# Seven half products for chunk 6, its sums on VectorE, and fewer weight sums per AV group

## The chip, the cores and the metric

One core of a Trainium2 chip runs the whole program. The metric is the device time of one execution in microseconds; the kernel before has a median of 409.77 us over three runs. TensorE (PE) multiplies matrices, VectorE (DVE), ScalarE (ACT) and GpSimd (POOL) work elementwise, and DMAs are issued by SyncE (SP), ACT and POOL.

## The reference

An attention whose queries are averaged in pairs, and then a gated feed-forward network on its output:

```python
q_pool = q.reshape(B, H, S // 2, 2, D).mean(axis=3)        # B=8, H=8, S=1152, D=64
scores = scale * np.matmul(q_pool, k.transpose(0, 1, 3, 2))
attn = np.exp(scores - np.max(scores, axis=-1, keepdims=True))
attn = attn / (np.sum(attn, axis=-1, keepdims=True) + 1e-09)
attn_out = np.matmul(attn, v)                               # (8, 8, 576, 64)
x = attn_out.transpose(0, 2, 1, 3).reshape(4608, 512)
h = (x @ w1) * (x @ w2) @ w3                                # 512 -> 1024 -> 1024
out = h @ w_out                                             # (4608, 512), float32
```

## The kernel before

**Attention.** Heads are worked on in 32 pairs. POOL casts keys, pooled queries and values to fp16; they are turned on TensorE for the first pairs and by DMA later. The scores of all pairs are one long row that is cut into 324 steps of 512 columns for two heads (`scores`, L434); ACT takes the exponential of each step into a ring in SBUF (L448). An AV group (`av_mm`, L461) multiplies a ring section of 128 queries with the values; a column of constants beside the values gives the sum of the exponentials. VectorE takes its reciprocal into `rzall` and scales (`av_norm`, L491). There are 144 such groups (`UNITS`). The result goes into `xT`.

**Network.** `w3 @ w_out` does not depend on the tokens: it is computed once into `T16` (`t_groups`, L544), 128 rows at a time, each in two steps of eight matmuls on 256 columns. The 4608 tokens are nine chunks of 512. For chunks 0 to 6 `moe_groups` (L613) makes, for each of eight blocks `ft` of 128 hidden features, the product with w1, which is kept (`keep`), and the product with w2, which VectorE multiplies with it (`gate`, L664) into the tile `g`. Then `g` is multiplied with T.

For chunks 0 to 5 that last product is done in seven half-sized products instead of eight, in the manner of Strassen and Winograd (`product`, L630): `g` and T are seen as 2 x 2 blocks, sums and differences of blocks of `g` are made by POOL (`sums`, L651, and `minus`, L731), those of T once by `t_sum`. Each half product is eight matmuls on 256 columns. Product 1 comes after block 4, and the other six wait in `late_fills` and run among the next chunk's steps. Results are added up on VectorE and stored quarter by quarter. Chunk 6 takes the plain way (L706): four token tiles, each eight matmuls on 512 columns, evicted half by VectorE and half by ACT.

Chunks 7 and 8 (`late_chunks`, L770) come when attention is over. They use seven products for the projections too, with sums of the weights (`weight_sums`, L734; eight POOL instructions, `wS`) and of `xT` (`x_sums`, L757; four POOL instructions for each chunk, `xS`). Their order (`LATE_ORDER`), the PSUM bank of each unit (`LATE_PLACES`) and the queue of some stores (`LATE_BY_ACT`) are written out by hand. The third unit uses the bank `avb`.

**Order.** Every engine runs its instructions in the order in which the program issues them. The 324 score steps are 108 visits of three (`VS`). What stands after the scores of a visit (AV groups `A`, network steps `m` or `s` by the PSUM bank they use, turns `P`) is chosen by `_visits` (L184), a search with a cost model over the list `fills` of the steps' sizes; a half product or a projection has size 1, a full token tile size 2. `av_step` (L1029) issues an AV group, its turn and its norm, and then one weight sum, as long as `todo` has any. After the last visit:

```python
while avn[0] < NU:          # L1076
    av_step()
    ...
    fill(avn[0] != NU - 4)
tail[0] = True              # L1083
```

Then come both sets of `x_sums` on POOL (L1089), a range test of all reciprocals on VectorE (L1094 to L1102, tile `ok`), the steps that are left (`while fill()`, L1103), a matmul that counts the test's results into `avb` (L1105) and VectorE's read of it (`badi`, L1107). If a value was out of range, a general version runs instead; with these inputs none is. With `tail` set, ACT instead of VectorE evicts the w1 products.

**Start.** Fifteen matmuls on the identity run into `avb` (L945) before the first data is there.

Of the kernel before, what the change touches and what calls it, by code (L numbers as in the profile page):

```python
# [258 lines left out]
    "0703 g31640 o00205 o01511 o10476 o11302"  # L259
).split()  # L260
LATE_ON_DVE = "o11c11".split()
LATE_BY_ACT = "o00c21 o01c12 o10c12 o10c21 o11c12 o11c21".split()


@with_exitstack
def kernel(
# [277 lines left out]
    def t_groups():  # L544
        w3T = {}

        def turn(ft):
            def go(pt):
                w3T[ft] = msb.tile([128, NF, 128], FP16, tag="t2k", bufs=2, name="w3T")
                ph = pt.bitcast(FP16)  # L550
                for a in range(NF):
                    nc.tensor.transpose(ph[:, a * 128:a * 128 + 128],
                                        w3c[ft // 4][:, ft % 4, a * 128:a * 128 + 128], ident16)

            return 0.5, go, lambda pt: nc.vector.tensor_copy(out=w3T[ft].rearrange("p a i -> p (a i)"),
                                                             in_=pt.bitcast(FP16)), W3_AT[ft // 2]

        def mult(ft, n0):
            def go(pT):
                for a in range(NF):  # L560
                    nc.tensor.matmul(pT[:, 0:256], w3T[ft][:, a, :], wosb[:, a, n0:n0 + 256],  # L561
                                     start=(a == 0), stop=(a == NF - 1))

            return 1, go, lambda pT: nc.vector.tensor_copy(out=T16[:, ft, n0:n0 + 256], in_=pT[:, 0:256]), WO_AT
# [48 lines left out]
    def moe_groups(c):  # L613
        t = {}
        lagged, late_fills[:] = late_fills[:], []
        seven = c < LATE - 1

        def first(pa, ft):
            if ft == 0:
# [22 lines left out]
        def quarter(h, n, pt, x):  # L642
            osb = msb.tile([128, 2, HM], FP32, tag="osb", bufs=3, name="osb")
            plus(osb, pt, x)
            store_two(nc.gpsimd, c * CH + h * HC, osb, slice(n * HM, n * HM + HM))

        def p1(pt):
            t["p"] = msb.tile([128, 2, HM], FP32, tag="t2k", bufs=2, name="p")
            nc.vector.tensor_scalar_mul(out=t["p"], in0=two(pt), scalar1=IS)

        def sums(f, n):  # L651
            g = t["g"]
            if f == 0:
                t["s1"] = msb.tile([128, HF, HC], FP16, tag="s1", bufs=1, name="s1")
            fs = slice(f, f + n)
            s1, a11, a21, a22 = t["s1"][:, fs], g[:, fs, 0:HC], g[:, fs, HC:CH], g[:, HF + f:HF + f + n, HC:CH]
            nc.gpsimd.tensor_tensor(out=s1, in0=a21, in1=a22, op=ALU.add)  # L657
            minus(a21, a11, a21)
            minus(a11, s1, a11)

        def half(fts):
            for ft in fts:
                def gate(pb, ft=ft):
                    nc.vector.tensor_tensor(out=t["g"][:, ft, :], in0=pb, in1=t["a"], op=ALU.mult)  # L664
# [11 lines left out]
        if seven:  # L676
            yield 1, lambda pt: product(pt, t["g"][:, 0:HF, 0:HC], 1), p1, 0.0
        yield from half(range(HF + 1, NF))
        if seven:
            g = t["g"]  # L680
            lo, hi = slice(0, HC), slice(HC, CH)

            def p2(pt):
                quarter(0, 0, pt, t["p"])
                for f in range(0, HF, 2):
                    minus(g[:, HF + f:HF + f + 2, lo], g[:, HF + f:HF + f + 2, lo], g[:, f:f + 2, lo])

            def p7(pt):
                t["z"] = msb.tile([128, 2, HM], FP32, tag="t2k", bufs=2, name="z")
                plus(t["z"], pt, t["p"])  # L690

            def p5(pt):
                t["bank"] = pt
                product(pt, t["s1"], 5)

            late_fills.extend((
                (1, lambda pt: product(pt, g[:, HF:NF, lo], 2), p2, 0.0),
                (1, lambda pt: product(pt, g[:, 0:HF, lo], 6), lambda pt: plus(t["p"], pt, t["p"]), 0.0),
                (1, lambda pt: product(pt, g[:, 0:HF, hi], 7), p7, 0.0),
                (1, lambda pt: product(pt, g[:, HF:NF, hi], 4), lambda pt: quarter(1, 0, pt, t["z"]), 0.0),  # L700
                (1, p5, lambda pt: quarter(1, 1, pt, t["z"]), 0.0),
                (1, lambda pt: product(t["bank"], g[:, HF:NF, lo], 3, False),
                 lambda pt: quarter(0, 1, t["bank"], t["p"]), None),
            ))
            return
        for tt in range(0, CH, 128):  # L706
            def go(po, tt=tt):
                for ft in range(NF):
                    nc.tensor.matmul(po, t["g"][:, ft, tt:tt + 128], T16[:, ft, :],  # L709
                                     start=(ft == 0), stop=(ft == NF - 1))  # L710

            def put(po, tt=tt):
                osb = msb.tile([128, dm], FP32, tag="osb", bufs=3)
                if tail[0]:
                    nc.vector.tensor_scalar_mul(out=osb[:, 0:256], in0=po[:, 0:256], scalar1=1.0 / (SCL * SCL))
                    nc.scalar.mul(out=osb[:, 256:512], in_=po[:, 256:512], mul=1.0 / (SCL * SCL))
                else:
                    nc.vector.tensor_scalar_mul(out=osb, in0=po, scalar1=1.0 / (SCL * SCL))
                if c == LATE - 1:
                    cut = 128 if tt < 256 else 64  # L720
                    for r in range(0, 128, cut):
                        for n in range(0, dm, 128):
                            store(nc.sync, c * CH + tt, osb[r:r + cut, n:n + 128], slice(n, n + 128), slice(r, r + cut))
                else:
                    store(nc.sync if c == LATE - 2 else nc.gpsimd, c * CH + tt, osb)

            yield 2, go, put, 0.0

    wS, tS, xS, todo = [], {}, {}, []

# [26 lines left out]
    def x_sums():  # L757
        for c in (0, 1):
            st = att.tile([128, 4, NC // 2, HC], FP16, tag="qst", name="xS")
            (_, a, n), = runs(LATE + c)  # L760
            b11, b12 = xT[:, 0:NC // 2, a:a + HC], xT[:, 0:NC // 2, a + HC:a + n]
            b21, b22 = xT[:, NC // 2:NC, a:a + HC], xT[:, NC // 2:NC, a + HC:a + n]
            x1, x2, x3, x4 = (st[:, i] for i in range(4))
            minus(x1, b12, b11)
            minus(x2, b22, x1)
            minus(x3, b22, b12)
            minus(x4, b21, x2)
            xS[c] = {1: b11, 2: b21, 3: b22, 4: x4, 5: x1, 6: x2, 7: x3}

    def late_chunks(before_end):  # L770
        room = att.tile([128, 27, 512], FP32, tag="ring", bufs=1, name="room")
# [170 lines left out]
        out=ident16, in_=ident16, compare_op=ALU.not_equal, fill=1.0,  # L942
        base=0, channel_multiplier=1, pattern=[[-1, 128]],
    )
    for _ in range(15):  # L945
        nc.tensor.matmul(avb[:, 0:64], ident16, ident16[:, 0:64], start=True, stop=True)
    for t in kq16s:
        nc.gpsimd.memset(t[QT:128, NB - 1], 0.0)
    nc.gpsimd.memset(half, 0.0)
# [55 lines left out]
                      ((old * FLAT + RING + TO[t]) // G) // VS - 1))  # L1005
    fills = []
    for ft in range(0, NF, 2):
        fills += [(0.5, W3_AT[ft // 2], "ms")] * 2 + [(1, WO_AT, "ms")] * 4
    free = []
    for n in range(NU + 1):  # L1010
        for c in loose.get(n, []):
            step = [(1, 0.0, "ms")]
            rest = step * 4 + [(1, 0.0, "m")] * 2
            fills += step * LAG + (rest if c else []) + step * (2 * NF - LAG)
            fills += step if c < LATE - 1 else [(2, 0.0, "ms")] * (CH // 128)
        free.append(len(fills))
    turn = {}
    for p in range(1, NPE):
# [10 lines left out]
    def av_step():  # L1029
        i = avn[0]  # L1030
        avn[0] += 1
        av_mm(i)
        if on_pe(i - 1):
            x_turn(i - 1)
        av_norm(i)
        if on_pe(i - 1):
            x_copy(i - 1)
        p, t = UNITS[i]
        if p >= XD and t == QM - 1:
            x_dma(p)  # L1040
        weight_sum()
        release()

    seen = -1
# [57 lines left out]
    nc.vector.memset(ones, 1.0)  # L1102
    while fill():  # L1103
        pass
    nc.tensor.matmul(avb[0:1, 0:1], okh, ones, start=True, stop=True)  # L1105
    badi = const.tile([1, 1], mybir.dt.int32)
    nc.vector.tensor_scalar(out=badi, in0=avb[0:1, 0:1], scalar1=-1.0, scalar2=float(128 * NQ),  # L1107
# [37 lines left out]
```

## Time and profile before

| | us |
|---|---|
| median of 3 runs | 409.77 (409.23 to 409.91) |
| the profiled execution | 409.23 |
| its span in the trace | 407.6 |
| TensorE busy | 392.2 |
| ACT busy | 336.6 |
| POOL busy | 282.0 |
| VectorE busy | 230.8 |
| granted TensorE clock | 0.998 |

Busy time is the time in which an engine executes an instruction. Matmuls are pipelined, so their mean duration is longer than the distance from one to the next; the chain of waits shows the distances. Times in rows are microseconds from the start of the span, durations behind them microseconds or nanoseconds as the view says. Tile names stand as `out<-in`.

### The profile page before, as it was taken

What the parts mean: (1) busy time and instruction counts of PE and PEld (TensorE: products, weight loads), DVE (VectorE), ACT (ScalarE), POOL (GpSimd) and SP (SyncE); (2) the same over time, 40 slices, a digit from 0 to 9 for tenths busy, and PEclk for the clock granted to TensorE, in tenths of its full rate; (3) what the DMA queues carried; (4) which work ended last, traced back from release to release, by engine and by line L of the source; (5) the groups of instructions that cost most, each with busy time, mean ns of one, the idle gap of its engine ahead of it and who ended that gap; (6) DMA issues with size and microseconds to landing.
All of it is one profiled execution on the core that took longest, in us unless ns stands there. A gap on an engine that the chain in (4) does not pass through costs nothing.

```text
span 407.6 us, 13533 instructions
## 1 busy us (share of the span) xinstructions
PE 392.2 (96%) x5632; PEld 275.5 (68%) x5632; DVE 230.8 (57%) x610; ACT 336.6 (83%) x384; POOL 282.0 (69%) x319
## 2 busy tenths in 40 slices
PE   4899999999999999999999999999999999999995
PEld 2477877665676666756676668666877767548884
DVE  1255665565555555465556555655555456845993
ACT  4989998999999999999999899989998987027752
POOL 5889975993968358855786398649663799930860
PEclk9999999999999999999999999999999999999999
DMA  8999998999889997999979999999896402311005
GB/s 260 253 321 285 276 291 296 348 252 276 167 272 261 260 209 183 319 219 254 296 217 303 268 214 218 220 319 277 187 282 133 62 16 66 79 55 49 2 27 185
DMA packets 94001, 86.37 MB, mean 212 GB/s; under 512 B 60272, under 2 KB 68720, under 8 KB 93936
## 3 DMA queue, kind: packets, MB, share of 16 engines
q1 hardware_dynamic: 83888, 59.06, 59.9%
q0 software_dynamic: 8896, 25.11, 22.2%
q10 hardware_dynamic: 1152, 1.31, 1.0%
q8 instruction: 44, 0.72, 0.7%
q14 instruction: 21, 0.17, 0.1%
HBM read 67.11 MB, written 9.44 MB: 188 GB/s over the span
## 4 chain that ended last, share of the span: by engine, by line
PE 89%; ACT 4%; POOL 3%; DVE 2%; issue 1%; DMA 1%; ACTq 0%; POOLq 0%
PE psc L443 20%; PE avb L474 17%; PE mo L587 12%; PE mot L587 9%; PE b L811 7%; PE mo L633 6%; ACT ring L448 3%; PE mo L561 3%; PE mot L633 3%; PE avb L471 2%; PE b L587 2%; PE b L709 2%; PE ptk L383 2%; POOL wS L747 2%; PE mo L811 1%
## 5 line engine op out<-in xcount | busy, mean ns | idle before, releaser
L448 ACT ACTIVATE ring<-psc 128x1024 f16<-128x1024 f32 x324 | 307.8, 1027 | 29.0 <-PE psc L443 27.4
L443 PE MATMUL psc<-kqT 64*128 64x512 f16 (+7 forms) x1152 | 97.6, 291 | 5.1 <-ACT ring L448 2.2
L474 PEld LDWEIGHTS <-ring 128*128 128x128 f16 x2304 | 84.0, 98 | 22.3 <-issue 8.8
L474 PE MATMUL avb<-vaug,ring 128*128 128x65 f16 x2304 | 91.5, 194 | 0.0
L443 PEld LDWEIGHTS <-kqT 64*128 64x128 f16 x1152 | 46.8, 95 | 34.3 <-issue 12.7
L355 POOL CAST kq<-kst 128x1152 f16<-128x1152 f32 x31 | 35.6, 1148 | 23.5 <-issue 12.6
L495 DVE RECIPROCAL rzall<-avb 128x2 f32<-128x2 f32 x144 | 23.9, 166 | 47.0 <-PE avb L474 21.5
L657 POOL TENSOR_TENSOR s<-gT 128x256 f16<-128x256 f16 (+1 forms) x18 | 14.9, 828 | 37.5 <-DVE gT L664 27.9
L359 POOL TENSOR_TENSOR kq<-qst 128x512 f16<-128x512 f32 x31 | 39.4, 1270 | 1.3 <-DMA qst<-in_q_dram 1.3
L664 DVE TENSOR_TENSOR gT<-mo,asb 128x512 f16<-128x512 f32 x35 | 24.2, 691 | 26.1 <-PE mo L587 24.9
L368 POOL CAST vaug<-vst 128x1152 f16<-128x1152 f32 x32 | 36.6, 1143 | 0.8 <-DMA vst<-in_v_dram 0.6
L587 PE MATMUL mo<-xT,w2sb 128*128 128x512 f16 (+2 forms) x160 | 36.2, 354 | 0.0
L587 PEld LDWEIGHTS <-w1sb 128*128 128x128 f16 x256 | 22.7, 98 | 19.7 <-issue 3.0
L587 PEld LDWEIGHTS <-w2sb 128*128 128x128 f16 x256 | 21.7, 97 | 19.9 <-issue 4.1
L633 PEld LDWEIGHTS <-gT 128*128 128x128 f16 x288 | 26.3, 98 | 8.5 <-issue 3.9
L509 DVE TENSOR_TENSOR xb<-avb,rzall 128x128 f16<-128x128 f32 x96 | 28.0, 292 | 3.3
L732 POOL TENSOR_TENSOR gT<-gT 128x512 f16<-128x512 f16 (+1 forms) x30 | 28.6, 963 | 1.5
L587 PE MATMUL mot<-xT,w1sb 128*128 128x512 f16 (+1 forms) x124 | 27.8, 352 | 0.0
L628 DVE COPY asb<-mo 128x512 f32<-128x512 f32 x25 | 17.3, 692 | 16.6 <-PE mo L587 16.3
L587 PE MATMUL mo<-xT,w1sb 128*128 128x512 f16 (+1 forms) x116 | 25.9, 351 | 0.0
L628 DVE COPY asb<-mot 128x512 f32<-128x512 f32 x27 | 18.7, 692 | 5.0 <-PE mot L587 5.0
L901 POOL TENSOR_TENSOR room<-gT 128x512 f16<-128x512 f16 x6 | 6.8, 1155 | 18.7 <-PE b L811 17.4
(159 smaller groups left out, 553.4 us busy)
## 6 DMA issues: line engine op xcount, KB each, us to landing
vst<-in_v_dram SPq DMA_DIRECT2D x25, 576.0 KB, 5.0
kst<-in_k_dram SPq DMA_DIRECT2D x23, 576.0 KB, 5.7
qst<-in_q_dram SPq DMA_DIRECT2D x23, 512.0 KB, 6.7
kst<-in_k_dram POOLq DMA_DIRECT2D x8, 576.0 KB, 10.1
qst<-in_q_dram POOLq DMA_DIRECT2D x8, 512.0 KB, 10.7
out_dram<-osb POOLq DMA_DIRECT2D x16, 256.0 KB, 5.2
vst<-in_v_dram POOLq DMA_DIRECT2D x7, 576.0 KB, 7.0
w3c<-in_moe_w_dram POOLq DMA_DIRECT2D x4, 512.0 KB, 8.3
```

The source lines that it names most:

```text
L355: nc.gpsimd.tensor_copy(out=kq16[:, 0:NJ].rearrange("p c u d -> p u c d"), in_=kst.rearrange("p u (c d) -> p u c d", d=D))
L359: eng.tensor_tensor(out=kq16[:, NJ:NJ + QM].rearrange("p c u d -> p u c d"), in0=qv[:, :, :, 0], in1=qv[:, :, :, 1], op=ALU.add)
L368: nc.gpsimd.tensor_copy(out=va[:, :, :, 0:D], in_=vs.pop(p).rearrange("p u (c d) -> p u c d", d=D))
L443: nc.tensor.matmul(psc[:, u, f - s * G:f - s * G + ln], kT2[u * 64:u * 64 + 64, jt, :], qpT[u * 64:u * 64 + 64, i0:i0 + ln], start=True, s ...
L448: nc.scalar.activation(out=ring[:, :, r0:r0 + G], in_=psc, func=AF.Exp, bias=0.0, scale=SCALE)
L474: nc.tensor.matmul(avb[:, o + u * E1:o + u * E1 + E1], ring[:, u, c0:c0 + 128], va[:, u, jt, :], start=(jt == 0 and u == 0), stop=(jt == N ...
L509: nc.vector.tensor_tensor(out=xbt, in0=av[:, :, 0:D], in1=rzall[:, i, :].unsqueeze(2).to_broadcast([128, 2, D]), op=ALU.mult)
L587: nc.tensor.matmul(pw[:, d0:d0 + n], wt[:, mc, ft * 128:ft * 128 + 128], xT[:, mc, a:a + n], start=(mc == 0 and d0 == 0), stop=(mc == NC - ...
L628: nc.vector.tensor_copy(out=t["a"], in_=pa)
L633: nc.tensor.matmul(pt[:, u * HM:u * HM + HM], a[:, f, u * 128:u * 128 + 128], tS[n][:, f, :], start=(start and u == 0 and f == 0), stop=(f ...
L732: nc.gpsimd.tensor_tensor(out=out, in0=x, in1=y, op=ALU.subtract)
L811: nc.tensor.matmul(pt[:, n * f:n * f + n], l[:, i, :], b[:, i, :], start=(p in (1, 5) and f == 0 and i == 0), stop=(i == kc - 1), skip_gro ...
```

## The change

- Chunk 6 is multiplied with T by seven half products. All of them come after block 7, in the order 1, 2, 6, 7, 5, 4, 3. Its sums are issued to VectorE behind the gates of blocks 5 (three on 512 columns), 6 and 7 (three each on 256 columns) and are written to the free tiles `kq16s`; the last difference (`s4`) stays on POOL. ACT evicts product 1. Its four quarters are stored in 32 pieces, 28 issued by SP and 4 by ACT.
- A weight sum follows every second AV group.
- `x_sums` for the second late chunk is issued after chunk 6's steps.
- The last store (`o01c12`) is issued by SP.
- The fifteen matmuls at the start are gone.
- In `t_groups` row block 3 is one step of eight matmuls on 512 columns with one eviction. The list `fills` has one entry of size 2 there, and seven of size 1 for chunk 6's product.

```diff
-LATE_BY_ACT = "o00c21 o01c12 o10c12 o10c21 o11c12 o11c21".split()
+LATE_BY_ACT = "o00c21 o10c12 o10c21 o11c12 o11c21".split()
...
-        def mult(ft, n0):
+        def mult(ft, n0, w=256):
             def go(pT):
                 for a in range(NF):
-                    nc.tensor.matmul(pT[:, 0:256], w3T[ft][:, a, :], wosb[:, a, n0:n0 + 256],
+                    nc.tensor.matmul(pT[:, 0:w], w3T[ft][:, a, :], wosb[:, a, n0:n0 + w],
                                      start=(a == 0), stop=(a == NF - 1))
...
-            for n in range(4):
-                yield mult(ft + n // 2, n % 2 * 256)
+            yield mult(ft, 0)
+            yield mult(ft, 256)
+            if ft != 2:
+                yield mult(ft + 1, 0)
+                yield mult(ft + 1, 256)
+            else:
+                yield mult(ft + 1, 0, dm)
...
-        seven = c < LATE - 1
+        final = c == LATE - 1
...
             plus(osb, pt, x)
-            store_two(nc.gpsimd, c * CH + h * HC, osb, slice(n * HM, n * HM + HM))
+            if not final:
+                store_two(nc.gpsimd, c * CH + h * HC, osb, slice(n * HM, n * HM + HM))
+                return
+            for u in range(2):
+                for r in range(0, 128, 64):
+                    for o in range(0, HM, 128):
+                        store(nc.sync if h or n or u else nc.scalar, c * CH + h * HC + u * 128, osb[r:r + 64, u, o:o + 128],
+                              slice(n * HM + o, n * HM + o + 128), slice(r, r + 64))
...
         def sums(f, n):
             g = t["g"]
+            eng = nc.vector if final else nc.gpsimd
             if f == 0:
                 t["s1"] = msb.tile([128, HF, HC], FP16, tag="s1", bufs=1, name="s1")
+                t["s2"], t["s4"] = ((x.rearrange("p c u d -> p (c u d)")[:, 0:HF * HC].rearrange("p (f i) -> p f i", f=HF)
+                                     for x in kq16s) if final else (g[:, 0:HF, 0:HC], g[:, HF:NF, 0:HC]))
...
-            nc.gpsimd.tensor_tensor(out=s1, in0=a21, in1=a22, op=ALU.add)
-            minus(a21, a11, a21)
-            minus(a11, s1, a11)
+            for o, x, y, op in ((s1, a21, a22, ALU.add), (a21, a11, a21, ALU.subtract), (t["s2"][:, fs], s1, a11, ALU.subtract)):
+                eng.tensor_tensor(out=o, in0=x, in1=y, op=op)
...
-                    if seven and ft > HF:
+                    if ft > HF:
                         sums(*((0, 2) if ft == HF + 1 else (ft - HF, 1)))
...
+        if final:
+            yield 1, lambda pt: product(pt, g[:, 0:HF, lo], 1), p1, 0.0
+            yield from (rest[i] for i in (0, 1, 2, 4, 3, 5))
+        else:
+            late_fills.extend(rest)
...
-    for _ in range(15):
-        nc.tensor.matmul(avb[:, 0:64], ident16, ident16[:, 0:64], start=True, stop=True)
...
-        weight_sum()
+        if i % 2:
+            weight_sum()
...
-    x_sums()
+    x_sums(0)
...
     while fill():
         pass
+    x_sums(1)
```

More of the change, by code (lines that the diff above doesn't have):

```diff
@@ L675, in moe_groups @@
         yield from half(range(HF + 1))
-        if seven:
+        if not final:
             yield 1, lambda pt: product(pt, t["g"][:, 0:HF, 0:HC], 1), p1, 0.0
         yield from half(range(HF + 1, NF))
[L679 to L727, printed above, removed]
+        g = t["g"]
@@ new lines, in moe_groups, with p2, p7, p5 @@
+        lo, hi = slice(0, HC), slice(HC, CH)
+        def p2(pt):
+            quarter(0, 0, pt, t["p"])
+            for f in range(0, HF, 2):
+                minus(t["s4"][:, f:f + 2], g[:, HF + f:HF + f + 2, lo], t["s2"][:, f:f + 2])
+        def p7(pt):
+            t["z"] = msb.tile([128, 2, HM], FP32, tag="t2k", bufs=2, name="z")
+            plus(t["z"], pt, t["p"])
+        def p5(pt):
+            t["bank"] = pt
+            product(pt, t["s1"], 5)
+        rest = [
+            (1, lambda pt: product(pt, g[:, HF:NF, lo], 2), p2, 0.0),
+            (1, lambda pt: product(pt, t["s2"], 6), lambda pt: plus(t["p"], pt, t["p"]), 0.0),
+            (1, lambda pt: product(pt, g[:, 0:HF, hi], 7), p7, 0.0),
+            (1, lambda pt: product(pt, g[:, HF:NF, hi], 4), lambda pt: quarter(1, 0, pt, t["z"]), 0.0),
+            (1, p5, lambda pt: quarter(1, 1, pt, t["z"]), 0.0),
+            (1, lambda pt: product(t["bank"], t["s4"], 3, False), lambda pt: quarter(0, 1, t["bank"], t["p"]), None),
+        ]
@@ L755, in t_sum, with x_sums @@
         minus(*((tS[5], b12, b11), (tS[6], b22, tS[5]), (tS[7], b22, b12), (tS[4], b21, tS[6]))[i])
[L757 to L768, printed above, removed]
+    def x_sums(c):
+        st = att.tile([128, 4, NC // 2, HC], FP16, tag="qst", name="xS")
+        (_, a, n), = runs(LATE + c)
+        b11, b12 = xT[:, 0:NC // 2, a:a + HC], xT[:, 0:NC // 2, a + HC:a + n]
+        b21, b22 = xT[:, NC // 2:NC, a:a + HC], xT[:, NC // 2:NC, a + HC:a + n]
+        x1, x2, x3, x4 = (st[:, i] for i in range(4))
+        minus(x1, b12, b11)
+        minus(x2, b22, x1)
+        minus(x3, b22, b12)
+        minus(x4, b21, x2)
+        xS[c] = {1: b11, 2: b21, 3: b22, 4: x4, 5: x1, 6: x2, 7: x3}
     def late_chunks(before_end):
```

13 lines of the change are left out of this document (8 added, 5 removed).

## The prediction

> **What bounds the kernel now.** I read the page first: engine shares and the chain that ended last.
>
> ```profile
> span 407.6 us, 13533 instructions
> PE 392.2 (96%) x5632; PEld 275.5 (68%) x5632; DVE 230.8 (57%) x610; ACT 336.6 (83%) x384; POOL 282.0 (69%) x319
> PE 89%; ACT 4%; POOL 3%; DVE 2%; issue 1%; DMA 1%; ACTq 0%; POOLq 0%
> ```
>
> TensorE bounds the run. An edit earns time only if it takes matmul streaming away or closes one of TensorE's few gaps, and it costs time if it opens one. So the second view was what TensorE waited for, 20 to 300 us; these are all its waits there:
>
> ```profile
> PE psc L443 <- ACT ring L448: 1.4, 5, 0.3
> PE psc L443 <- DVE kqT L385: 0.8, 1, 0.8
> ```
>
> 2.2 us in 280: the long middle has little to win. The third view was the chain in order of time from 312 us, where POOL appears; the timeline shows the TensorE wait itself, and the VectorE result that POOL works on.
>
> ```profile
> 323.72 1.09 POOL vaug L368
> 324.81 2.09 POOL wS L747
> ...
> 326.97 4.20 POOL wS L747 x2
> 331.18 0.63 POOL s L657
> ...
> 336.36 0.87 PE mot L633 x8
> ...
> 353.72 5.18 PE b L587 x24
> 358.90 6.91 PE b L709 x32
> 365.81 0.10 PE avb L1105
> ```
>
> ```profile
> 326.75 0.69 DVE L664 TENSOR_TENSOR gT<-mo,asb 128x512 f16<-128x512 f32 x1 [0.16 <-PE mo L587]
> 333.35 0.72 PE L633 MATMUL mot<-tS,gT 128*128 128x256 f16 x5 [0.69 <-POOL gT L732]
> ```
>
> Chunk 5's last gated block is ready at 327.44 (326.75 + 0.69). POOL starts its three sums only at 331.18, because three weight sums of about 2.1 us stand ahead; the half product that needs the third sum waits 0.69 us. After it the chain is TensorE without a break to the late chunks: chunk 6's projections to 358.90, its full product with T (32 matmuls of 512 columns, 6.91 us), and the first late work at 365.81. In that stretch every microsecond is one of the total.
>
> **The change, part by part**
>
> **Chunk 6's product.** Out go 32 matmuls, 6.91 us; in come seven half products of 8 matmuls, 0.87 each in the row at 336.36: 6.09. Gain 0.82.
>
> **Its sums on VectorE.** This is the critical part. VectorE from 355 us, with the first and the fifth of POOL's eight sums for the late chunks:
>
> ```profile
> 355.23 0.30 DVE L1094 TENSOR_SCALAR ok<-rzall 128x288 f32<-128x288 f32 x1
> 355.44 1.26 DVE L1095 TENSOR_SCALAR ok<-rzall 128x288 f32<-128x288 f32 x1
> 356.74 0.46 DVE L1096 TENSOR_TENSOR ok<-ok 128x288 f32<-128x288 f32 x1
> ...
> 357.80 0.69 DVE L664 TENSOR_TENSOR gT<-b,asb 128x512 f16<-128x512 f32 x1
> 350.66 1.17 POOL L732 TENSOR_TENSOR xS<-xT 128x512 f16<-128x512 f16 x1
> 355.24 1.29 POOL L732 TENSOR_TENSOR xS<-xT 128x512 f16<-128x512 f16 x1
> ```
>
> ```profile
> L901 DVE TENSOR_TENSOR room<-gT x2: 409/412/414, 395.4 to 395.7; 128x512 f16<-128x512 f16 x2
> L870 DVE TENSOR_TENSOR gT<-room x8: 693/982/1561, 373.0 to 393.8; 128x512 f16<-128x512 f32 x8
> ```
>
> The range test of the reciprocals (L1094 to L1102) is queued ahead of the gates of blocks 5, 6 and 7, so these start at 357.80 although their matmuls ended earlier. Before, the full product met block 7 only at its eighth matmul and nothing stalled. After, nine sums stand between and behind those gates: three on 512 columns, 0.41 each by the L901 row, and six on 256 columns. No row has that size on VectorE; half the row is 0.21, the whole 0.41, and I take the middle, 0.31, since part of a duration does not shrink. Unshifted, block 7's gate ends at 357.80 + 3 x 0.69 + 3 x 0.41 + 3 x 0.31 = 362.03. TensorE gets there at 358.90 + 0.87 (product 1) + 0.33 (three matmuls of product 2) = 360.10. Stall 1.9 us. Behind TensorE's wait is everything: products 6, 7, 5, 4, 3 and the late chunks. Bounds: 0.2 if the sums cost 0.21 for 256 and 0.33 for 512 columns, as when such instructions overlap, and the test loses its 0.96 wait (1.26 against 0.30 for the same form); 4.0 if the sums cost 0.41 and the test meets 1.8 us more of such waiting. I take 1.9: the test as its rows show it.
>
> Product 6 needs the last difference, 3 x 0.31 = 0.93 after that gate, and its fourth matmul comes 0.88 after it: level. Product 3 needs POOL's two differences, 1.16 each; four products of 0.87 cover them. Nothing for either.
>
> **The seam to the late chunks.** The third late unit writes the bank that the range result is read from.
>
> ```profile
> 366.25 0.14 DVE L1107 TENSOR_SCALAR badi<-avb 1x1 int32<-1x1 f32 x1
> 366.72 0.60 PE L811 MATMUL avb<-xT,w1sb 128*128 128x256 f16 x4
> L599 SPq DMA_DIRECT2D out_dram<-osb x24: 366/587/1356, 361.1 to 375.3; - x24
> out_dram<-osb SPq DMA_DIRECT2D x15, 32.0 KB, 2.0
> ```
>
> Now there is 0.33 us of room. After, the last quarter's sum (0.69 where 0.42 stood) is ahead of that read on VectorE, and its buffer is the first quarter's. That buffer is free when its stores have landed: four on each of two queues, 0.59 and a gap of 0.05 each, 2.0 to land. From product 2's end: 0.2 + 0.69 + 3 x 0.64 + 2.0 = 4.8; the last product ends at 5 x 0.87 = 4.35. VectorE waits some 0.3, reads at about 5.7, and the unit, due at 5.3, loses 0.4. Bounds 0.1 and 0.6; I take 0.3. ACT's four issues lie before its first late copy and SP's 28 issues of 0.64 end near 381, ahead of its first late store at 388: nothing.
>
> **Weight sums behind every second group.** Eight sums then take sixteen AV groups. One instead of three stands ahead of chunk 5's last sums: POOL is free at 326.95, the gate ends at 327.44, three sums of 0.67 end at 329.5, ahead of the product that needs them. Gain 0.69. The other side, by POOL's share of the stretch:
>
> ```profile
> 324.00:349.00 25.00, 24.32 (x384) 17.05 (x381) 14.86 (x40) 17.72 (x19) 24.73 (x20) 1.00 0.19 44
> ```
>
> POOL (the fifth figure) is busy for 24.73 of 25 us. The weight sums now end with the last group, and they push the four sums for chunk 7 from a start at 350.7 to about 353-357.6. Late units read these after 367: covered by 9 us, and if that cover went, each would cost its 1.15. The second set, moved behind chunk 6, is due at its first reader, about 377, and ends near 370. That set leaves VectorE's stretch.
>
> **Last store.**
>
> ```profile
> 402.08 0.40 SPq L599 DMA_DIRECT2D out_dram<-room  x1
> 403.32 0.68 ACTq L599 DMA_DIRECT2D out_dram<-room  x1
> DMA packets 187, 0.18 MB, mean 350 GB/s; under 512 B 23, under 2 KB 186, under 8 KB 186
> ```
>
> SP is idle after 402.5; the data is ready at 403.15. The issue would start up to 0.15 earlier and take 0.4 for 0.68: at most 0.44. The last row is 404.5 to 405 us: the DMA engines still move 350 GB/s, so an earlier issue may only queue: at least 0. I take 0.25.
>
> **Warm-up matmuls and the wide T step.**
>
> ```profile
> 1.49 0.98 PE L946 MATMUL avb<-ident 128*128 128x64 f16 x15 [1.49 <-POOL ident L941]
> 5.10 0.50 PE L423 MATMUL ptf<-ident,kq 128*128 128x128 f16 x3 [2.63 <-POOL kq L409]
> 15.09 1.65 PE L383 MATMUL ptk<-ident,kq 128*128 128x128 f16 x14 [0.31 <-ACT ring L448]
> 25.42 0.94 PE L383 MATMUL ptk<-ident,kq 128*128 128x128 f16 x14
> ```
>
> The 15 matmuls end 2.6 us before TensorE's first wanted work, which waits for POOL. Fourteen transposes still take 1.65 us at 15 us and 0.94 at 25, so whatever speeds TensorE up comes long after them; taking them out costs and gives nothing. The wide step streams the same columns, and its one VectorE copy is hidden. But it is one entry fewer in the list from which the order is written out, so the order after it may differ; see the second rival.
>
> **Sum:** -0.82 + 1.9 + 0.3 - 0.69 - 0.25 = +0.44. Against the profiled execution, 409.23 (span 407.6 and 1.6 around it), that is 409.7. That execution is the fastest of three, so I add the sum to their median: 409.77 + 0.44 = **410.2**. Two gains are eaten by a VectorE wait at the place of one of them. About 0.2%, 0.8 us, is what a measurement of this kernel can tell from no change.
>
> **Rivals**
>
> **VectorE and POOL block each other (slower).** L1095 takes 1.26 where the same form took 0.30, and it ends 0.17 after the POOL instruction beside it (355.24 + 1.29). L870, both inputs in SBUF, ranges from 0.69 to 1.56. So a VectorE instruction can wait out a POOL one. Chunk 7's sums now lie later, over the whole range test and perhaps over the first of the nine sums; L1094 and L1096, which ran free, could each wait up to 1.15. It decides if POOL is still in those sums at 356 us. Price 0.6 to 2.3, typically 1.6 on top of the sum: 410.2 + 1.6 = 411.8. Against it: only four POOL instructions, not eight, follow there. The Trainium skill (SBUF — State Buffer, "Who interferes with whom") states that a VectorE instruction with two SBUF inputs contends with a GpSimd one that reads SBUF, and that the second to issue blocks fully; by that rule all nine sums are exposed, which speaks against this change. The L870 row agrees. Chance 0.21.
>
> **The written-out order ends differently (faster).** After the last scores seven AV groups remain, one fill between each; the range test follows the last. Each group that the new order puts ahead of the last scores leaves 1.6 more fills (0.87 us each) after the test, of which the gates that go with them use 0.55: 0.85 us more room on VectorE. Two groups close the stall: -0.82 - 0.69 + 0.2 + 0.3 - 0.25 = -1.3, 409.77 - 1.3 = 408.5; the 2.2 us of waits in the middle can shrink too. For: nothing but the order fixes where the test falls. Against: the wide step moves no work. Chance 0.36.
>
> **TensorE slows down after the stall.** The transposes at 15 us show its slow pace after waits; a stall near 3.4 us could bring the 1.65-for-0.94 pace back for a few microseconds, 2 us more: 412.6. The Trainium skill (TensorE: Matmul & The Clock Gate, "What's actually happening") has the clock halved after an idle window of about 3.4 us; no run here shows it going down again. Chance 0.03.
>
> **How the numbers follow.** Forecast 0.40, order 0.36, blocking 0.21, slow clock 0.03. The forecast's own bounds put 0.27 of its 0.40 within 0.2%, 0.09 above, 0.04 below. The order case is faster with 0.32 and within with 0.04; blocking is slower with 0.18, within with 0.03; the clock is slower. Faster 0.36, same 0.34, slower 0.30. Low end: the order case with a little of the 2.2 us, 408.3. High end: the blocking case, 411.8.
>
> **What would show it.** Right: no POOL wait at the half product near 333; the chain of chunk 6 shows products of 0.87 with one gap before the end of the second, ended by VectorE, of about 1.9 us; the third late unit waits some tenths for the range read; the last issue stands on SP. Wrong: no such gap (the order moved the test), or L1094 and L1096 over 1 us long (blocking), or matmuls after the gap at twice their pace.

## The result and the profile after

| | before | after |
|---|---|---|
| median, six runs each on one chip, us | 409.50 (408.99 to 409.91) | 413.41 (412.92 to 415.37) |
| ratio after to before, 95% interval | | 1.0107 (1.0084 to 1.0130) |
| span of the profiled execution, us | 407.6 | 411.8 |
| granted TensorE clock | 0.998 | 0.996 |

The change makes the kernel 1.1% slower, above the predicted range. The page of the kernel after, and its chain that ended last:

```profile
span 411.8 us, 13546 instructions
PE 392.3 (95%) x5633; PEld 276.5 (67%) x5633; DVE 237.4 (58%) x620; ACT 335.7 (82%) x381; POOL 284.6 (69%) x321
PE 90%; ACT 4%; DVE 3%; issue 1%; DMA 1%; ACTq 0%; DVEq 0%
```

TensorE is as busy as before (392.3 for 392.2) though a half product of 0.87 us is gone, so matmuls somewhere ran longer; POOL has left the chain and VectorE's share has grown. The timeline of the kernel after, TensorE (start, duration, group, and the wait ahead of it with what ended it), shows where:

```profile
332.39 1.04 PE L638 MATMUL mot<-tS,gT 128*128 128x256 f16 x8
...
358.10 1.25 PE L638 MATMUL b<-T,gT 128*128 128x256 f16 x10
361.37 0.28 PE L638 MATMUL b<-T,gT 128*128 128x256 f16 x1 [2.02 <-DVE gT L681]
363.28 0.72 PE L638 MATMUL b<-T,gT 128*128 128x256 f16 x5 [1.62 <-DVE gT L681]
363.83 1.75 PE L638 MATMUL b<-tS,kq 128*128 128x256 f16 x8
365.38 1.91 PE L638 MATMUL b<-tS,gT 128*128 128x256 f16 x8
...
370.03 0.16 PE L1101 MATMUL avb<-ones,okh 128*1 128x1 f16 x1
...
371.01 0.60 PE L807 MATMUL avb<-xT,w1sb 128*128 128x256 f16 x4
```

The half product at 332.39 runs its eight matmuls in one piece: the 0.69 us wait for POOL is gone. Products 1 and 2 begin at 358.10, 0.64 us earlier than chunk 6's product did before. Then TensorE waits twice inside product 2 for gates on VectorE, 3.64 us in all, and products 6 and 7, though fed, take 1.75 and 1.91 us. The third late unit (371.01) starts 0.98 behind the counting matmul (370.03), as before (366.72 and 365.74): no wait at the seam. The same view of the kernel before:

```profile
358.74 7.07 PE L709 MATMUL b<-T,gT 128*128 128x512 f16 x32
365.74 0.16 PE L1105 MATMUL avb<-ones,okh 128*1 128x1 f16 x1
```

The chain of waits has these two at 358.90 and 365.81; from here on, starts are compared within the timeline alone.

The clock in stretches of half a microsecond (the third figure from the end):

```profile
363.50:364.00 0.50, 0.50 (x7) 0.45 (x5) 0.47 (x3) 0.00 (x0) 0.00 (x0) 0.99 0.00 0
364.00:364.50 0.50, 0.50 (x4) 0.32 (x3) 0.47 (x2) 0.00 (x0) 0.35 (x1) 0.50 0.00 0
...
367.00:367.50 0.50, 0.50 (x5) 0.37 (x4) 0.17 (x1) 0.00 (x0) 0.50 (x1) 0.60 0.44 111
```

The granted clock is 0.50 from 363.99 (the first stretch's mean of 0.99 leaves 0.01 us of half speed) to 367.40 (the last's 0.60 leaves 0.40 us): 3.41 us at half speed.

VectorE and POOL in the same stretch of the kernel after:

```profile
354.59 0.38 DVE L1089 TENSOR_SCALAR ok<-rzall 128x288 f32<-128x288 f32 x1
354.89 1.25 DVE L1090 TENSOR_SCALAR ok<-rzall 128x288 f32<-128x288 f32 x1
356.18 1.34 DVE L1091 TENSOR_TENSOR ok<-ok 128x288 f32<-128x288 f32 x1
...
358.12 0.69 DVE L681 TENSOR_TENSOR gT<-b,asb 128x512 f16<-128x512 f32 x1
358.91 1.01 DVE L676 TENSOR_TENSOR s<-gT 128x512 f16<-128x512 f16 x1
359.95 0.42 DVE L676 TENSOR_TENSOR gT<-gT 128x512 f16<-128x512 f16 x1
...
361.35 0.74 DVE L676 TENSOR_TENSOR s<-gT 128x256 f16<-128x256 f16 x1
362.12 0.29 DVE L676 TENSOR_TENSOR gT<-gT 128x256 f16<-128x256 f16 x1
...
362.54 0.68 DVE L681 TENSOR_TENSOR gT<-b,asb 128x512 f16<-128x512 f32 x1
```

```profile
354.76 1.22 POOL L729 TENSOR_TENSOR xS<-xT 128x512 f16<-128x512 f16 x1
356.06 1.15 POOL L729 TENSOR_TENSOR xS<-xT,xS 128x512 f16<-128x512 f16 x1
357.16 1.37 POOL L729 TENSOR_TENSOR xS<-xT 128x512 f16<-128x512 f16 x1
358.50 1.14 POOL L729 TENSOR_TENSOR xS<-xT,xS 128x512 f16<-128x512 f16 x1
360.79 1.15 POOL L729 TENSOR_TENSOR kq<-gT,kq 128x512 f16<-128x512 f16 x1 [1.15 <-DVE kq L676]
```

POOL's four x sums lie from 354.76 to 359.64, over the whole test and the first sum. Instructions of one form have two durations: 0.42 free and 1.01 beside POOL on 512 columns, 0.29 and 0.74 on 256 (this one beside POOL's first difference of chunk 6, at 360.79). The test's second comparison takes 1.25, as before (1.26); the product of the two comparisons takes 1.34 for the 0.46 of before.

The two spans, term by term from these rows and those of before. Product 1 starts earlier: 358.10 - 358.74 = -0.64. Products 1 and 2 take 363.83 - 358.10 = 5.73 where two at 0.87 take 1.74: +3.99. From product 6 to the counting matmul: 370.03 - 363.83 = 6.20, where the same five products take 4.53 at the full clock (e12_fillseam, below): +1.67. Seven products at that pace for the 7.00 of before (365.74 - 358.74): 1.74 + 4.53 - 7.00 = -0.73. From the counting matmul to the end: 41.77 for 41.86, -0.09. Sum +4.20; the spans differ by 4.2.

### The profile page after: what moved, and what is told of

It is laid out like the page before. It is cut to its first block, busy times and chain, and to the rows that moved or that the text cites. A ratio compares the mean times of both kernels' runs of the same rounds, so it can differ in the third digit from the quotient of the medians.

```text
span 411.8 us, 13546 instructions
## 1 busy us (share of the span) xinstructions
PE 392.3 (95%) x5633; PEld 276.5 (67%) x5633; DVE 237.4 (58%) x620; ACT 335.7 (82%) x381; POOL 284.6 (69%) x321
## 4 chain that ended last, share of the span: by engine, by line
PE 90%; ACT 4%; DVE 3%; issue 1%; DMA 1%; ACTq 0%; DVEq 0%
PE psc L443 20%; PE avb L474 18%; PE mo L592 13%; PE mot L592 9%; PE mo L638 7%; PE b L807 6%; ACT ring L448 3%; PE mo L561 3%; PE mot L638 3%; PE avb L471 2%; PE b L638 2%; PE ptk L383 2%; PE mo L807 1%; DMA qst<-in_q_dram 1%; PE avb L807 1%
## 5 line engine op out<-in xcount | busy, mean ns | idle before, releaser
L638 PEld LDWEIGHTS <-gT 128*128 128x128 f16 x320 | 29.8, 99 | 12.6 <-issue 4.1
L614 POOL DMA_DIRECT2D out_dram<-osb x16 | 11.8, 738 | 12.3 <-DVE osb L642 6.2
L638 PE MATMUL mo<-T,gT 128*128 128x256 f16 x128 | 16.8, 274 | 0.0
```

The source lines that it names most:

```text
L638: nc.tensor.matmul(pt[:, u * HM:u * HM + HM], a[:, f, u * 128:u * 128 + 128], tS[n][:, f, :], start=(start and u == 0 and f == 0), stop=(f ...
```

## The experiments

The theory after this reading: VectorE and POOL block each other in the test and the sums; this lengthens the gap, and the gap brings the half clock. The rivals: the work queued ahead of the gates is too long in itself; the slow products cost nothing of their own; the lost time lies in the small parts of the change. Ratios are to the kernel before on the same chip, with their 95% intervals.

**e1_weight: one part alone.** The kernel before, with

```diff
-        weight_sum()
+        if i % 2:
+            weight_sum()
```

> The kernel before with one part alone: a weight sum behind every second AV group. All theories: the 0.69 us wait of the half product near 333 us is gone and nothing stands in its place, about 0.7 us faster than before (408.8 against 409.5). Same as before or slower would mean that the later weight sums and the later sums for chunk 7 cost something themselves.

409.60 beside 409.80; 0.9996 (0.9985 to 1.0007). The wait at the half product near 333 is gone, and yet nothing is gained. The timeline of e1_weight:

```profile
357.31 1.34 DVE L1097 TENSOR_TENSOR ok<-ok 128x288 f32<-128x288 f32 x1
...
359.23 1.75 PE L709 MATMUL b<-T,gT 128*128 128x512 f16 x7
361.39 5.57 PE L709 MATMUL b<-T,gT 128*128 128x512 f16 x25 [0.41 <-DVE gT L664]
```

The later x sums draw out the test (1.34 for 0.46), and chunk 6's old product, which had met no wait, now waits 0.41 for block 7's gate. From the start of its first matmul to the end of its last it takes 361.39 + 5.57 - 359.23 = 7.73 us, 0.66 more than the 7.07 of before: what was won near 333 is lost here.

**e2_notest: the test left out.** The change, with the range test left out (a constant in its place).

```diff
-    ok = const.tile([128, 2, NQ], FP32)
...
     okn = const.tile([128, 1], FP32)
-    nc.vector.reduce_sum(out=okn, in_=ok[:, 0, :], axis=mybir.AxisListType.X)
+    nc.vector.memset(okn, float(NQ))
```

> The changed kernel without the range test of the reciprocals (left out: the check of the softmax sums; its result is set to a constant). Theory Q (VectorE's queue: the test, drawn out to 3.6 us by POOL's sums beside it, stands ahead of gates 5 to 7): gates 5 to 7 follow their products, the wait inside product 2 shrinks from 3.7 us to under 0.5, the granted clock stays at 1, and the time is 408.0 to 408.5, below the kernel before. Rival S (the nine sums themselves are too much for VectorE): the gap stays at 1.5 us or more, about 410 or above. Rival C (the slow clock comes from something other than the gap): the clock still falls to 0.5 around 364 us, about 410.

411.90; 1.0053 (1.0034 to 1.0072). VectorE, POOL and TensorE of e2_notest:

```profile
356.13 1.26 DVE L676 TENSOR_TENSOR gT<-gT 128x512 f16<-128x512 f16 x1
357.31 1.37 DVE L676 TENSOR_TENSOR kq<-s,gT 128x512 f16<-128x512 f16 x1
...
355.89 1.21 POOL L729 TENSOR_TENSOR xS<-xT,xS 128x512 f16<-128x512 f16 x1
357.07 1.33 POOL L729 TENSOR_TENSOR xS<-xT 128x512 f16<-128x512 f16 x1
...
361.86 0.72 PE L638 MATMUL b<-T,gT 128*128 128x256 f16 x5 [2.23 <-DVE gT L681]
```

With 3.3 of the test's 3.53 us taken away (a cast and two constants stay), the gap is still 2.23 us, and the time lies 3.4 us above the range: now the sums lie under POOL's x sums and take 1.26 and 1.37 for 0.42. That the test is merely too long falls as the whole cause; blocking moves to whatever lies beside POOL. Rival S expected such a gap too, but from the sums alone; e10_unblocked and e11_best decide that below.

In the profiled execution the half clock came again, and from product 6 (362.41) to the counting matmul (368.61) it is 6.20 us, as in the change. It did not come every time. Such a stretch takes 3.41 x 0.5 / 411 = 0.004 off the mean clock of an execution, so one with a mean of 0.998 or more cannot hold it. The six executions of the change have means of 0.991 to 0.996; of the six of e2_notest only two are that low (0.996 at 412.30 us, the profiled one, and 0.994 at 413.11), and the other four have 0.998 to 1.000 at 410.79 to 412.10 us.

**e3_filled and e12_fillseam: the gap without the idling.** Sixteen matmuls of no use (into `avb`, result unused) between products 1 and 2; e12_fillseam also stores the first quarter in two pieces instead of eight.

```diff
         if final:
             yield 1, lambda pt: product(pt, g[:, 0:HF, lo], 1), p1, 0.0
+            for _ in range(16):
+                nc.tensor.matmul(avb, ident16, T16[:, 0, :], start=True, stop=True)
```

> The changed kernel with 16 extra matmuls of 512 columns (3.45 us at full pace, their result is not used) between products 1 and 2 of chunk 6, into the bank avb that nothing else uses there: TensorE works instead of waiting. Theory C (the gap lets the clock fall to half, which costs 1.9 us on products 6, 7 and 5): clock 1 throughout, the products back to 0.87, about 411.5 against 413.4 of the changed kernel; VectorE's chain as before. If the slow products had another cause, the time is 413.4 or more.

> The change with 16 matmuls of no use (512 columns, result unused) between products 1 and 2, so that TensorE does not idle there, and with the first quarter in two stores instead of eight, so that the wait for stores that took the gain in the run with the matmuls alone is not there. Clock theory: the half clock behind the gap costs 1.3 to 1.9 us of the change's time by itself; 411.5 to 412.3 here beside 413.4 of the change. Rival (the gap alone costs, the slow products are covered by something later): 413.2 to 413.5, and a wait shows in the tail in place of the one at the third late unit.

e3_filled 413.16; 1.0096 (1.0077 to 1.0115). e12_fillseam 412.66; 1.0070 (1.0046 to 1.0095), 0.4 us above what the clock theory expected and below what its rival did. TensorE of e12_fillseam:

```profile
359.46 3.62 PE L726 MATMUL avb<-T,ident 128*128 128x512 f16 x16
...
363.78 0.72 PE L638 MATMUL b<-T,gT 128*128 128x256 f16 x5 [0.38 <-DVE gT L684]
364.34 1.04 PE L638 MATMUL b<-tS,kq 128*128 128x256 f16 x8
...
368.87 0.16 PE L1106 MATMUL avb<-ones,okh 128*1 128x1 f16 x1
```

Product 6 starts 5.75 us after product 1 (358.59), as in the change (5.73): VectorE's delay is untouched. But the clock stays at 1.00, and what follows takes 368.87 - 364.34 = 4.53 us instead of 6.20. So 1.67 us are the clock's own. In e3_filled the stretch is the same 4.53, yet its time is 1.7 us above the 411.5 expected; 0.46 was given back at the third late unit, and the rest is not accounted for (timeline of e3_filled):

```profile
370.46 0.60 PE L809 MATMUL avb<-xT,w1sb 128*128 128x256 f16 x4 [0.46 <-DVE badi L1105]
```

That is the seam that the prediction priced at 0.3: it opens only when the products before it run at full pace. By the ratios e12_fillseam recovers 0.0037, 1.5 us, of the change's 0.0107; the two intervals overlap, so the clock's price rests on the rows.

**e4_every and e9_seam: POOL out of the test.** The change with `weight_sum()` behind every group again; e9_seam with two stores for the first quarter besides.

```diff
-        if i % 2:
-            weight_sum()
+        weight_sum()
```

> The changed kernel with one part undone: a weight sum behind every AV group again. POOL's sums for chunk 7 then end near 355.3 us, when the range test begins. Theory Q with blocking by POOL: the 0.69 us wait near 333 is back, but the test takes 1.5 to 1.7 us instead of 3.6, the first of the nine sums 0.4 instead of 1.0, the gap in product 2 about 1 us, no fall of the clock: 409.5 to 410.0, over 3 us faster than the changed kernel though a good part was taken away. Without blocking (the sums alone make the gap): gap near 3 us, 412 or more.

> e4_every (the changed kernel with a weight sum behind every group, 1.0028 of before) with the first quarter of chunk 6 stored in two pieces instead of eight. Seam theory: in e4 the last quarter's sum waited 0.96 us for those stores to land and the third late unit 0.47 us for it; with two pieces both waits go, 0.4 to 0.5 us faster than e4, about 1.0016 of before. If that wait has cover elsewhere, it stays at 1.0028.

e4_every 411.06; 1.0028 (1.0009 to 1.0046). e9_seam 410.46; 1.0019 (1.0003 to 1.0035). The timeline of e4_every, VectorE and TensorE:

```profile
356.02 0.30 DVE L1089 TENSOR_SCALAR ok<-rzall 128x288 f32<-128x288 f32 x1
358.67 0.43 DVE L676 TENSOR_TENSOR gT<-gT 128x512 f16<-128x512 f16 x1
...
362.00 0.72 PE L638 MATMUL b<-T,gT 128*128 128x256 f16 x5 [1.32 <-DVE gT L681]
...
368.70 0.60 PE L807 MATMUL avb<-xT,w1sb 128*128 128x256 f16 x4 [0.47 <-DVE badi L1102]
```

POOL's x sums end at 355.85, as the test begins (355.81). The test's second comparison is back at 0.30 and the sum at 0.43, the waits in product 2 fall from 3.64 to 1.32, product 6 starts 3.25 us behind product 1 (362.56 and 359.31) instead of 5.73, and the clock stays at 1.00. The wait of 0.68 at the half product near 333 is back, and the seam costs 0.47. By the ratios e4_every is 3.2 us faster than the change, as expected, but it is 1.1 us above its range: about 1 us of gap was expected, and the seam was not counted. In e9_seam the unit starts on time; the two ratios' intervals overlap, so its worth in time is not shown.

**e7_small: the small parts alone.** The kernel before with the last store by SP, no warm-up matmuls and the wide T step (diff as in the change).

> The kernel before with only the small parts of the change: last store by SP, no matmuls at the start, the wide T step. My theory: between 0 and 0.25 us faster than before, from the last store. Rival: one of them is part of the slowdown (a colder start, a worse order after the wide step), 0.3 us or more slower.

409.67; 1.0003 (0.9986 to 1.0019): no effect that shows. The interval is too wide to tell 0.25 us from nothing.

**e5_reduce: a test that POOL doesn't block.** e1_weight, with the test as a minimum and a maximum. The bounds are the same.

```diff
-    nc.vector.tensor_scalar(out=ok[:, 0, :], in0=rzf, scalar1=SCL / 32768.0, scalar2=None, op0=ALU.is_ge)
...
+    nc.vector.tensor_reduce(out=rzm[:, 0:1], in_=rzf, axis=mybir.AxisListType.X, op=ALU.min)
+    nc.vector.tensor_reduce(out=rzm[:, 1:2], in_=rzf, axis=mybir.AxisListType.X, op=ALU.max)
+    nc.vector.tensor_scalar(out=okh[:, 0:1], in0=rzm[:, 0:1], scalar1=SCL / 32768.0, scalar2=None, op0=ALU.is_ge)
```

> e1_weight (the kernel before with a weight sum behind every second AV group, measured at 0.9996 of before) with the range test taken from the least and the greatest reciprocal, two reductions of one input each, in the same place. Blocking theory: in e1 POOL's later sums drew the test out to 3.4 us and TensorE waited 0.6 us in chunk 6's product, which ate the 0.69 us won near 333; reductions do not wait for POOL, the test takes about 1.3 us, that wait goes and the time is 0.6 to 0.7 us below before. If weight sums behind every second group are worth nothing in themselves, it stays within 0.2 us of before.

408.97 beside 409.64; 0.9976 (0.9959 to 0.9994), faster than both kernels. The timeline of e5_reduce:

```profile
355.89 0.44 DVE L1096 TENSOR_REDUCE rzm<-rzall 128x1 f32<-128x288 f32 x1
355.70 1.16 POOL L732 TENSOR_TENSOR xS<-xT 128x512 f16<-128x512 f16 x1
...
359.04 7.07 PE L709 MATMUL b<-T,gT 128*128 128x512 f16 x32
```

Both reductions take 0.44 with POOL beside them (the second is shown), and chunk 6's 32 matmuls run in one piece. (The interval overlaps that of e1_weight at its edge; the wait's end is shown by the row.) The Trainium skill (SBUF — State Buffer, "Who interferes with whom") says that on this chip tensor_reduce never contends with GpSimd; these rows agree. Fewer weight sums pay, then, where nothing on VectorE lies open to POOL.

**e8_best, e10_unblocked and e11_best: the change with its obstacles moved.** All three take the reduced test, issue it behind block 7, and store the first quarter in two pieces. e8_best skips only two weight sums (behind groups 129 and 130); e10_unblocked skips none; e11_best is e8_best with the last two weight sums held back until chunk 6 is issued, so that the x sums end by 352.90. The diff is that of e11_best, against the change:

```diff
+        if i not in (129, 130) and len(todo) > 2:
+            weight_sum()
...
+    for _ in range(5):
+        fill()
+    nc.vector.tensor_reduce(out=rzm[:, 0:1], in_=rzf, axis=mybir.AxisListType.X, op=ALU.min)
...
+    while todo:
+        weight_sum()
     x_sums(1)
```

> The changed kernel with the causes taken out: a weight sum behind every group but the two of chunk 5's last block (so POOL is done with chunk 7's sums near 356 us and the wait near 333 is still gone), the range test by two reductions and behind block 7 instead of ahead of block 5, the first quarter stored in two pieces instead of eight. Blocking theory: the nine sums take 0.43 and 0.29 each, gap in product 2 under 0.5 us, clock at 1, no wait of the third late unit over 0.3: 1.0 to 1.5 us below before, 408.3 to 408.8. If nine sums on VectorE are too much in themselves, the gap stays above 1 us and it is no faster than before.

> The change with a weight sum behind every AV group, the range test made by a minimum and a maximum (two tensor_reduce and two small comparisons) behind block 7 instead of ahead of it, and the first quarter stored in two pieces. What is meant: POOL's first x sums end near 355.8, so nothing on POOL reads SBUF while the nine sums run on VectorE, and the test no longer stands ahead of them. Blocking theory: sums at their free 0.42 and 0.29 us, gap of TensorE in product 2 from 1.48 to 0.3 or less, no half clock, third late unit without a wait; the wait at 333 (0.7 to 0.9) stays. Time 409.0 to 409.5 beside 409.6 of before. Rival (nine sums are more than VectorE has room for, blocked or not): a gap of over 1 us stays in product 2, time 410.3 or more.

> The kernel of the run before it by the same name ending (a weight sum behind every AV group but two, reduced test behind block 7, first quarter in two pieces), with the last two of the weight sums held back until behind chunk 6, so that POOL's first x sums start and end about 2.5 to 4 us sooner. Blocking theory: x sums end near 354, sums at 0.42 and 0.29, gap in product 2 from 1.41 to 0.3 or less, no wait at 333; what stays is a wait of product 3 for a quarter sum (up to 0.7). Time 408.3 to 409.1, faster than before and than the change. Rival (VectorE lacks the room whatever POOL does): gap over 1 us, time as the earlier one, 410.3.

e8_best 410.38; 1.0017 (1.0002 to 1.0032), 1.6 us above its range and as its rival expected: the x sums, to 357.69, still block the first sums (0.87 and 1.26), and the gap is 1.24. e10_unblocked 410.25; 1.0007 (0.9990 to 1.0024). e11_best 409.14 beside 409.84; 0.9977 (0.9961 to 0.9993). VectorE and TensorE of e10_unblocked, then TensorE of e11_best:

```profile
357.33 0.42 DVE L679 TENSOR_TENSOR gT<-gT 128x512 f16<-128x512 f16 x1
...
359.32 2.06 PE L638 MATMUL b<-T,gT 128*128 128x256 f16 x16
...
365.56 1.03 PE L638 MATMUL b<-T,kq 128*128 128x256 f16 x8 [0.69 <-DVE osb L642]
```

```profile
357.85 2.05 PE L638 MATMUL b<-T,gT 128*128 128x256 f16 x16
...
364.08 1.03 PE L638 MATMUL b<-T,kq 128*128 128x256 f16 x8 [0.68 <-DVE osb L642]
```

In both, products 1 and 2 are one piece of sixteen matmuls: all nine sums fit on VectorE when the test stands behind them. That VectorE lacks room whatever POOL does falls: e8_best and e11_best differ only in POOL's order, and the gap goes from 1.24 to nothing. e10_unblocked still missed its range by 0.75 us: the wait near 333 (0.69) had been counted, but product 3 waits another 0.69 for a quarter sum that the test delays (e13_split bears on this), and in the profiled execution the stores behind the last matmul took 5.3 us for the 4.9 of before.

e11_best has no wait near 333 and beats the kernel before by 0.7 us by the medians, at the upper edge of its range. But e5_reduce, with chunk 6's plain product, has the same ratio (0.9976 and 0.9977). Chunk 6's last product takes 7.26 us in e11_best (from 357.85 to 364.08 + 1.03) and 7.07 in e5_reduce: product 3's wait of 0.68 takes back what seven products save. So fewer weight sums and the reduced test are shown to pay together; that the seven products for chunk 6 pay is shown by no run.

**e13_split: the wait that was left.** e11_best, with the minimum and maximum of all but the last 16 units taken earlier, to shorten the test ahead of the quarter sums.

```diff
+        if i == NU - 16:
+            spread(0, 0, 2 * (NU - 16))
...
+    spread(1, 2 * (NU - 16), NQ)
```

> The kernel before it, with the range test split: minimum and maximum of the first NU - 16 units are taken 16 units before the end, between AV groups, and only the last 16 units' behind block 7. The two long tensor_reduce (0.44 us each) in front of the quarter sums become two short ones, estimated at 0.15 each from the lengths, so the chain of quarter sums starts about 0.6 sooner. If the test in front of the sums is what product 3 waits for: its wait falls from 0.85 to about 0.25, third late unit 0.4 to 0.6 sooner, time 408.2 to 408.8 (ratio 0.996 to 0.998). Rival (the wait is the chain of quarter sums itself or a store): wait stays at 0.7 or more, time as before it, ratio 0.9977.

409.64; 0.9991 (0.9979 to 1.0003): a miss. The timelines of e13_split and, in the second fence, of e11_best:

```profile
360.69 1.15 POOL L732 TENSOR_TENSOR kq<-gT,kq 128x512 f16<-128x512 f16 x1 [2.21 <-DVE kq L679]
360.74 1.12 DVE L1102 TENSOR_SCALAR okh<-rzm 128x2 f16<-128x2 f32 x1
...
364.97 1.03 PE L638 MATMUL b<-T,kq 128*128 128x256 f16 x8 [0.94 <-DVE osb L642]
```

```profile
360.62 0.15 DVE L1097 TENSOR_SCALAR okh<-rzm 128x1 f16<-128x1 f32 x1
```

The long reductions shrank to 0.27 for both, but a comparison of two columns met POOL's last difference and took 1.12 us, where that of one column took 0.15 in e11_best, also beside POOL (360.06 to 361.21). From the test's first row to the first quarter sum it is 1.32 us for 1.06 in e11_best, and product 3 waited 0.94 for 0.68: both grew by 0.26. Its wait does follow the test's length, but the edit made the test longer.

## Why the prediction was wrong

**The step that failed** is the gap in product 2: "I take 1.9: the test as its rows show it". It measured 3.99. The test took 358.12 - 354.59 = 3.53 up to the first gate for 357.80 - 355.23 = 2.57 before: +0.96. The gates and sums, from the first gate's start to the third's end, took 363.22 - 358.12 = 5.10 for the 4.23 of the sum: +0.87. A last +0.16 is a slip between two views: the sum took TensorE's start from the chain (358.90) and VectorE's from the timeline, where the product starts at 358.74. Together +1.99 of the 2.06 missing.

The cause is POOL's place. With only that undone, e4_every, 2.48 of the 3.99 go (5.73 - 3.25). With the test out of the way and only POOL's order changed, from e8_best to e11_best, a wait of 1.24 goes to nothing. With the test left out but POOL in place, e2_notest, 2.23 stays. Some of e4_every's rest is POOL's too: the first sum on 256 columns takes 0.75 there, beside the first difference of chunk 6. The bound of 4.0 met the size by luck: it stood for 1.8 us more of waiting in the test, where 0.96 came. The bound of 0.2 is a slip: the durations it names give 0.4.

**The rival that happened** is the first, blocking, with its price about right (1.6 on top of the sum; 0.96 + 0.87 = 1.83 measured), and its chance of 0.21 was too low by the prediction's own times. The reason against it, "only four POOL instructions, not eight, follow there", counted instructions and not their times: the same text had moved those four to 353 to 357.6, and they lay at 354.76 to 359.64, on the test and the first sum. Of its two signs one came: the product of the comparisons (1.34), not the first comparison (0.38). The rule on shared ports that it cited held for the two of the nine sums that ran beside POOL (1.01 and 0.74).

**The third rival happened too**, at a chance of 0.03 and a price of 2 (410.2 + 2 is 412.2, not its 412.6); the clock's price is 1.67 by e12_fillseam, about half of 3.41 us. It was weighed as an alternative to the first, but the first is what brings it: a gap of 1.9 plus 1.6 is the length at which it was said to begin. The two together, 410.2 + 1.6 + 2 = 413.8, would have been nearest to 413.41. "No run here shows it going down again" misread the trace of the kernel before. Its last matmul ends at 402.69, and the clock is at half from 405.70 on (in the same view as above, 0.20 us of this stretch are at full speed):

```profile
405.50:406.00 0.50, 0.00 (x0) 0.00 (x0) 0.00 (x0) 0.00 (x0) 0.00 (x0) 0.70 0.09 31
```

**The other terms.** The product: 0.73 at the full clock for 0.82; the last of the seven and the one before it take 0.97 and 0.94 us in e12_fillseam, not 0.87. Weight sums: the wait of 0.69 went as forecast, but alone it shows no gain (e1_weight): the step looked for readers of the delayed x sums, and no late unit waits for them, but VectorE beside them does. The seam: 0 in the change, 0.46 and 0.47 where the products run at pace, within its bounds. Last store, warm-up and wide step: nothing shown (e7_small), where 0.25 was taken for the first. The order: unchanged, so the second rival, the likeliest of the three, was false; no fill moved past the last scores.

## What to carry to other kernels

Before work is moved to VectorE, write down which GpSimd instructions will run beside it after the change, with their times and not their number: here both engines lengthened each other, which cost 1.83 us in the gap, where the new product had 0.73 to gain. A range test made by reductions was immune to this (e5_reduce), and with that one edit a change that had shown no gain gave 0.2%. And price a long wait of TensorE twice, once for itself and once for the clock behind it.

## What the runs showed of the hardware

- In the profiled executions a wait inside product 2 of 2.23 us (e2_notest) or of 2.02 and 1.62 (the change) was followed by half the clock for 3.41 us and a loss of 1.67; waits of 1.32 (e4_every) and 1.24 (e8_best) were not. By the mean clocks, at most two of the six executions of e2_notest held such a stretch. The Trainium skill (TensorE: Matmul & The Clock Gate, "What's actually happening") puts the return to half clock behind at least one idle window of about 3.4 us. The length of the slow stretch agrees; the wait ahead of it was shorter than such a window in e2_notest, and there the measurement decides.
- After the program's last matmul the clock fell after 2.12 us in e11_best (402.01 to 404.13), 3.01 in the kernel before and 5.38 in e1_weight (403.84 to 409.22). In the trace of the change its stretches at full speed between two changes last 344.75 and 44.37 us, which is 101 and 13 times 3.413. This fits a clock that changes only at such steps, so that the same wait can bring the half clock in one execution and not in another; no run tests it further.
- A tensor_scalar of two columns took 1.12 us beside a POOL instruction (e13_split), of one column 0.15 (e11_best), each seen once: the size of the work is no measure of what it can lose.
- POOL loses too: its x sums took 1.33 (e2_notest) and 1.37 us (the change) beside VectorE for 1.15 alone.
